# Both phases of a two-layer kernel in halves of d_ff, seven products for eight in three of the four, and converted weights kept in DRAM

## The chip, the cores and the metric

The kernel runs on one core of one Trainium2 chip. The metric is the device time of one execution in microseconds (us), as the median of several runs; smaller is better. The engines are TensorE (PE; PEld is its loading of the stationary operand), VectorE (DVE), ScalarE (ACT), GpSimd (POOL) and SyncE (SP), which issues nearly all DMAs.

## The reference

Three stages follow one another: sparse attention, then two two-layer networks with different activations. All is float32; the weights come as float64, two 32-bit words each.

```python
q, k, v: (4, 8, 576, 64)     # batch, heads, positions, head size
mask_local   = (rel >= 0) & (rel < 32)                     # heads 0 to 3; rel = query - key position
mask_strided = (rel >= 0) & (key % 32 == query % 32)       # heads 4 to 7
x = softmax(where(mask, q @ k.T / 8, -1e9)) @ v            # then (2304, 512)

h = x @ w_in                                               # first phase, w_in (512, 2048)
g = h where h >= 1, 0 where h <= -1, else (h + 1) ** 2 / 4
x = g @ w_out                                              # w_out (2048, 512)

h = x @ w2_in                                              # second phase, same shapes
out = (s * relu(h) ** 2 + b) @ w2_out
```

## The kernel before

**Tiles.** Tokens go in nine blocks `j` of 256 (`g` counts the blocks of both phases, 0 to 17), d_ff in eight pairs `p` of 128-wide tiles. One *step* is one layer of one block and one pair. The first layer (`layer1`, L831) takes 24 matmuls of 256 columns into one PSUM bank `h`: four chunks of d_model, two d_ff tiles, three products each, since every operand is split into a rounded part and a residual (`xh`, `xl`; `w[:, 0]`, `w[:, 1]`; `gh`, `gl`) and high x high, high x low and low x high are summed. `activate` (L846) makes `g`. The second layer of the first phase (`layer2`, L937) takes 24 more, with the weights stationary, into `y`, so its result comes out with d_model on the partitions. The second phase uses `layer2_fast` (L893): Strassen's scheme in Winograd's form on 2x2 blocks, seven products for eight, 21 matmuls a step. For it `combine` (L871) makes four sums `s1` to `s4` of quarters of `h` and `u`, `w_combine` (L707) the four differences `t1` to `t4` of the weights, and `finish_fast` (L908) adds up the seven results.

**Order of the work.** `PASSES` (L62) lists the block passes: (block, first pair, end). The second layer runs `LAG` = 2 pairs behind the first. In the first phase all sixteen d_ff tiles' weights are in SBUF; blocks 0 and 1 go two pairs at a time, blocks 2 to 5 in one pass of eight, blocks 6 to 8 in two halves. The second phase goes in halves: all its blocks with pairs 0 to 3, then with pairs 4 to 7. Where a block has several passes, the first phase stores each pass's result in DRAM (`x2`, L397) and adds them when the second phase loads them (`x_split`, L788); the second phase stores partial sums (`sums`) and adds them in `finish_fast`. Sixteen attention units (batch, pair of heads) run beside this from the step numbers in `STARTS` (L51); units listed in `MEMORY` borrow weight rooms.

**Weights.** Each of the 64 tiles is loaded by one DMA (`w_load`, L657) and converted from float64 by three VectorE operations (`w_bits`, L682) and split by one ScalarE copy and one subtraction (`w_parts`, L700). `W_TIMES` and `W_NEXT` (L73) give the step at which each tile's load is due; `pump` (L753) waits for free rooms (SBUF buffers of 4 KB a partition).

**Who sets the order.** The class `Order` records every operation with a due time (`nc.now`, in steps) and then orders them itself with prices of its own, each engine's queue separately; at each moment the ready operation with the earliest due time goes next. So all operations stand in the profile under the one line that issues them, L381, and are told apart by tile names. Every queue runs in its order: an operation that waits holds up all behind it on its engine, SyncE's DMAs included.

Of the kernel before, what the change touches and what calls it, by code (L numbers as in the profile page):

```python
# [67 lines left out]


AGAIN = (6, *range(9, 16))  # L70


W_TIMES = {0: (-7, 1.9, 3), 1: (7.9, 1.9, 2.6)}  # L73
W_NEXT = {0: (113, 1.4), 1: (150, 3.2)}
W_AHEAD, W_RETRY, W_GAP = 3, 0.5, 1.2
# [3 lines left out]
U_BANKS, W_BANKS = ("a0", "a1", "a2", "a3"), ("a3", "a2", "a1", "a0")  # L79
W_BANKS_FAST, Y_BANKS_FAST = ("a3", "a2"), ("y0", "y1", "a0", "a1")  # L80
# [35 lines left out]
class Order:  # L116
# [4 lines left out]
    BANKS = ("h0", "h1", "y0", "y1", "a0", "a1", "a2", "a3")  # L121

    def __init__(self, nc):
        self.nc, self.ops, self.place, self.count, self.seen, self.first = nc, [], {}, {}, {}, {}
        self.past = set()
        self.filler = []
        self.choices, self.uses = {}, {}
        self.tiles, self.shadow = {}, bacc.Bacc("TRN2", target_bir_lowering=False, num_devices=1)
        self.now = 0.0

        self.in_line, self.line = False, None
        for e in self.ENGINES:
            setattr(self, e, Order.Engine(self, e))
# [56 lines left out]
    def record(self, engine, op, args, kw):  # L190
# [28 lines left out]
        self.line = i if self.in_line else None  # L219
        deps.discard(i)  # L220
# [7 lines left out]
    def price(self, engine, op, out, aps, kw):  # L228
# [5 lines left out]
        if engine == "tensor":  # L234
            n = out.free_size()
            if op == "transpose":
                return n * 0.00085
            if aps[1].dtype == F32:
                return max(0.0255, 0.0004 * n)
            return n * 0.000453  # L240
        if engine == "scalar":
            return (0.17 if psum else 0.2) + 0.00083 * n + 0.09 * (isinstance(kw.get("bias"), bass.AP) + ("accum_out" in kw))
        if engine == "vector":
            return 0.15 + (0.00052 if self.fast(op, aps) else 0.00104) * n
        if engine == "gpsimd":
            return (0.25 + 0.0019 * n if n <= 512 else 0.12 + 0.0017 * n) if op != "memset" else 0.04 + 0.0009 * n
# [138 lines left out]
def attention_moe_moe(ctx, tc, q, k, v, w1_in, w1_out, w2_in, w2_out, s_in, b_in, consts, out):  # L385
# [10 lines left out]
    x2 = [  # L396
        [nc.tile(dram, [P, NC, N], F32, f"x2_{j}_{i}") for i in range(sum(g == j for g, _, _ in PASSES))] for j in range(NBLK)  # L397
    ]
# [11 lines left out]
    turns = [0]  # L410
# [11 lines left out]

    def put(b, copy, o, i):
# [6 lines left out]
    class Unit:  # L430


        def __init__(self, b, pair, mem, quick=False, natural=False):
            self.b, self.pair, self.mem, self.quick, self.natural = b, pair, mem, quick, natural
# [3 lines left out]
            self.id = f"{b}_{pair}"  # L438

# [45 lines left out]
        def load_v(self):  # L485
            queue = nc.gpsimd if self.quick and not self.strided else nc.sync
# [108 lines left out]
        def smul(self):  # L595
            nc.vector.tensor_tensor(
# [57 lines left out]
    rooms, half_rooms, halves = [], [], {}  # L654
    wt, wraw, wtags, reserved, used = {}, {}, {}, {}, {}

    def w_load(ph, f, x):  # L657
        w = ((w1_in, w1_out), (w2_in, w2_out))[ph][x]
        if ph == 0:
            tag = f"w{f}_{x}"  # L660
        else:
            tag = reserved[f // 2].pop(0) if x else rooms.pop(0)
        wtags[ph, f, x] = tag

        r = wraw[ph, f, x] = nc.tile(sb, [P, DM, 2], I32, tag=tag, name=f"wr{ph}_{f}_{x}")
        if x == 0:
            nc.sync.dma_start(
                out=r.rearrange("p (c m) w -> p c (m w)", m=P),
                in_=w[:, 2 * f * P:2 * (f + 1) * P].rearrange("(c p) m -> p c m", p=P),
            )  # L670
        else:
            nc.sync.dma_start(out=r.rearrange("p m w -> p (m w)"), in_=w[f * P:(f + 1) * P, :])


    wc = {}

    def w_abs(ph, f, x):
        c = nc.bank(ps, W_BANKS if now[0] < 2 * NP * NBLK - 4 else W_BANKS_FAST, f"c{ph}_{f}_{x}", "c")
        nc.scalar.activation(out=c, in_=wraw[ph, f, x][:, :, 1].bitcast(F32), func=AF.Abs, scale=REBIAS)
        wc[ph, f, x] = c  # L680

    def w_bits(ph, f, x):  # L682
        c, r = wc[ph, f, x].bitcast(I32), wraw[ph, f, x]
        o = wc[ph, f, x] = nc.tile(sb, [P, DM], I32, tag="wc", bufs=WC_BUFS, name=f"wc{ph}_{f}_{x}")
# [22 lines left out]
    def w_combine(p):  # L707

        r0, r1 = [wc.pop((1, 2 * p + f, 1)).bitcast(F32) for f in range(2)]
        b11, b12, b21, b22 = r0[:, :HM], r0[:, HM:], r1[:, :HM], r1[:, HM:]  # L710

        r = wraw[1, 2 * p + 1, 1].bitcast(F32).rearrange("p m w -> p (m w)")
# [4 lines left out]
        t, tags = {}, {0: wtags[1, 2 * p, 1], 1: reserved[p][2], 2: reserved[p][0], 3: reserved[p][1]}  # L717
        for i, c, eng in ((2, u, nc.vector), (3, w, nc.gpsimd), (0, r1, nc.gpsimd), (1, b11, nc.vector)):
            o = t[i] = w_room(tags[i], f"w1_{p}_{i}", c.free_size())
            nc.scalar.activation(out=o[:, 0], in_=c, func=AF.Copy)  # L720
            eng.tensor_tensor(out=o[:, 1], in0=c, in1=o[:, 0].bitcast(F32), op=ALU.subtract)
        b21, b22 = t[0][:, :, :HM], t[0][:, :, HM:]
        t1, t3, t2, t4 = t[2][:, :, :HM], t[2][:, :, HM:], t[3][:, :, :HM], t[3][:, :, HM:]
        wt[1, p] = dict(b11=t[1], b21=b21, b22=b22, t1=t1, t2=t2, t3=t3, t4=t4)
        rooms.append(wtags[1, 2 * p + 1, 1])
        used[1, p] += tags.values()

    def w_free(ph, p):
        for tag in used.pop((ph, p)):
            (half_rooms if tag in halves else rooms).append(tag)  # L730

    def plan_w(f):
        for x in range(2):
            first, step, apart = W_TIMES[f // (NF // 2)]
            t = first + step * (f % (NF // 2)) + apart * x
            at(t - W_AHEAD, w_load, 0, f, x)
            at(t, w_abs, 0, f, x)
            at(t, w_bits, 0, f, x)
            at(t + 0.3, w_parts, 0, f, x)

    todo = [
        (W_NEXT[p // HP][0] + W_NEXT[p // HP][1] * (4 * (p % HP) + 2 * x + f), (1, 2 * p + f, x))
        for p in range(NP) for x in range(2) for f in range(2)
    ]
    loaded = [0]

    def half_split(tag):
# [371 lines left out]
```

## Time and profile before

| | |
|---|---|
| median of 3 runs | 914.93 us (913.59 to 916.2) |
| the profiled execution's own time | 914.73 us |
| its span, first to last instruction | 913.0 us |
| mean granted TensorE clock | 0.987 |
| TensorE, VectorE, ScalarE, GpSimd busy | 886.8, 523.3, 495.9, 414.1 us |
| DMA | 103.37 MB, mean 113 GB/s |

The shares of busy time are means over unlike stretches, so what an engine's time is worth is read from a stretch and from who waits there. Matmuls overlap in the records, so their spacing, not their mean duration, is their cost.

### The profile page before, as it was taken

What the parts mean: (1) busy time and instruction counts of PE and PEld (TensorE: products, weight loads), DVE (VectorE), ACT (ScalarE), POOL (GpSimd) and SP (SyncE); (2) the same over time, 40 slices, a digit from 0 to 9 for tenths busy, and PEclk for the clock granted to TensorE, in tenths of its full rate; (3) what the DMA queues carried; (4) which work ended last, traced back from release to release, by engine and by line L of the source; (5) the groups of instructions that cost most, each with busy time, mean ns of one, the idle gap of its engine ahead of it and who ended that gap; (6) DMA issues with size and microseconds to landing.
All of it is one profiled execution on the core that took longest, in us unless ns stands there. A gap on an engine that the chain in (4) does not pass through costs nothing.

```text
span 913.0 us, 22147 instructions
## 1 busy us (share of the span) xinstructions
PE 886.8 (97%) x8922; PEld 872.8 (96%) x8922; DVE 523.3 (57%) x1057; ACT 495.9 (54%) x1097; POOL 414.1 (45%) x350
## 2 busy tenths in 40 slices
PE   8987999999999999999999999999999999999996
PEld 7987999999999999999999999999999899999996
DVE  2787686443443342333696888744457965455455
ACT  2676677545444443233554687665666655555553
POOL 4174454122222112222354577987645665545544
PEclk9999799999999999999999999999999999999999
DMA  9899322422222211002635743445134332222211
GB/s 161 258 300 309 89 75 71 103 52 52 64 52 63 53 61 70 1 24 70 209 127 172 232 140 116 145 136 183 70 115 164 98 129 99 94 93 93 94 47 47
DMA packets 122966, 103.37 MB, mean 113 GB/s; under 512 B 84272, under 2 KB 100976, under 8 KB 122864
## 3 DMA queue, kind: packets, MB, share of 16 engines
q1 hardware_dynamic: 122352, 100.85, 36.7%
q0 software_dynamic: 512, 1.11, 0.6%
q8 instruction: 70, 1.15, 0.5%
q14 instruction: 32, 0.26, 0.1%
HBM read 73.63 MB, written 28.31 MB: 112 GB/s over the span
## 4 chain that ended last, share of the span: by engine, by line
PE 87%; DMA 3%; DVE 3%; ACT 2%; POOL 2%; issue 2%; SPq 0%; POOLq 0%; DVEq 0%; ACTq 0%
PE h L381 40%; PE y L381 38%; PE s L381 3%; PE o L381 2%; PE idle L381 2%; DMA wr<-in_moe_w_out_dram 1%; POOL gl L381 1%; PE t L381 1%; PE p L381 1%; DMA x<-o 1%; DMA wr<-in_moe_w_in_dram 1%; DVE o L381 1%; ACT u L381 1%; POOL w L381 1%; DMA mem<-in_q_dram 1%
## 5 line engine op out<-in xcount | busy, mean ns | idle before, releaser
L381 PE MATMUL h<-xh,w 128*128 128x256 f32 x2304 | 436.3, 281 | 5.7 <-ACT xh L381 3.0
L381 PEld LDWEIGHTS h<-xh,w 128*128 128x128 f32 x2304 | 364.0, 189 | 7.4 <-ACT xh L381 3.1
L381 PE MATMUL h<-xl,w 128*128 128x256 f32 x1152 | 323.2, 281 | 0.0
L381 PE MATMUL y<-g,w 128*128 128x256 f32 x1728 | 221.9, 283 | 5.7 <-DVE o L381 5.7
L381 PEld LDWEIGHTS h<-xl,w 128*128 128x128 f32 x1152 | 217.4, 189 | 0.3
L381 PEld LDWEIGHTS y<-g,w 128*128 128x128 f32 x1728 | 210.8, 190 | 6.6 <-DVE o L381 5.8
L381 POOL TENSOR_TENSOR g<-u,g 128x512 fp32r<-128x512 f32 x72 | 95.4, 1324 | 246.3 <-ACT g L381 148.3
L381 PE MATMUL y<-w,g 128*128 128x256 f32 x864 | 158.2, 281 | 1.0 <-ACT w L381 1.0
L381 ACT ACTIVATE u<-h 128x512 f32<-128x512 f32 x144 | 85.9, 598 | 119.0 <-DVE h L381 55.5
L381 PEld LDWEIGHTS y<-w,g 128*128 128x128 f32 x864 | 132.3, 188 | 1.3 <-ACT w L381 1.3
L381 DVE TENSOR_SCALAR u<-h 128x512 f32<-128x512 f32 x72 | 49.6, 689 | 132.1 <-PE h L381 126.7
L381 POOL TENSOR_TENSOR gl<-u,g 128x384 fp32r<-128x384 f32 x72 | 75.1, 1043 | 100.8 <-ACT g L381 95.1
L381 PE MATMUL y<-w,gl 128*128 128x256 f32 x432 | 120.7, 281 | 0.0
L381 POOL TENSOR_TENSOR gl<-s,g 128x512 fp32r<-128x512 f32 x72 | 97.8, 1358 | 33.8 <-ACT g L381 31.5
L381 ACT ACTIVATE u<-u,half 128x512 f32<-128x512 f32 x72 | 52.0, 722 | 108.2 <-DVE u L381 106.9
L381 ACT ACTIVATE g<-u 128x512 fp32r<-128x512 f32 (+1 forms) x144 | 83.2, 578 | 36.5 <-DVE u L381 30.3
L381 DVE TENSOR_SCALAR h<-h,sbt 128x512 f32<-128x512 f32 x72 | 58.6, 814 | 69.6 <-ACT h L381 69.6
L381 POOL TENSOR_TENSOR w<-wc,w 128x512 fp32r<-128x512 f32 x56 | 74.0, 1327 | 43.5 <-ACT w L381 38.8
L381 PEld LDWEIGHTS y<-w,gl 128*128 128x128 f32 x432 | 81.0, 188 | 0.1
L381 DVE TENSOR_TENSOR o<-y,o 128x256 f32<-128x256 f32 x120 | 46.4, 415 | 41.5 <-PE y L381 40.0
L381 DVE TENSOR_TENSOR u<-h,u 128x512 f32<-128x512 f32 x72 | 49.3, 685 | 23.2 <-ACT u L381 23.1
L381 ACT ACTIVATE g<-s 128x512 fp32r<-128x512 f32 x72 | 45.3, 629 | 14.8 <-DVE s L381 14.8
(91 smaller groups left out, 995.9 us busy)
## 6 DMA issues: line engine op xcount, KB each, us to landing
wr<-in_moe_w_in_dram SPq DMA_DIRECT2D x32, 512.0 KB
wr<-in_moe_w_out_dram SPq DMA_DIRECT2D x32, 512.0 KB
x<-o SPq DMA_DIRECT2D x36, 256.0 KB
scratch<-x SPq DMA_DIRECT2D x18, 512.0 KB
y<-o SPq DMA_DIRECT2D x22, 256.0 KB
scratch<-y SPq DMA_DIRECT2D x11, 512.0 KB
out_dram<-o SPq DMA_DIRECT2D x18, 256.0 KB
xhd<-xh SPq DMA_DIRECT2D x8, 512.0 KB
```

The lines of the kernel that those rows point to most:

```text
L381: getattr(getattr(self.nc, engine), op)(*args, **kw)
```

## The change

The first phase too goes in halves of d_ff: a half `hp` is 0 or 1 in the first phase and 2 or 3 in the second, and in each half every block takes one pass of pairs 0 to 3 (blocks 0 and 1 of half 0 two pairs at a time). Of the 288 steps each half has 72.

- Half 0 keeps eight products, but with `g` stationary and the weights moving, 512 columns a matmul: 12 for 24. Half 1 uses `layer2_fast`, as the second phase does, so `combine` and `w_combine` run there too, and the max of the activation is written to `h`.
- Results of the first phase now have tokens on the partitions. Half 0's are stored as partial sums in DRAM; half 1's `finish` loads and adds them (on GpSimd), transposes 32x32 blocks on VectorE, and stores them in `x2` in pieces of 128 bytes, 72 DMAs of 64 KB in all. The second phase loads a block in four DMAs, with no addition; its `w_in` loads come in four DMAs of 32 partitions to match.
- At the start only half 0's weights are loaded. Of each later half the pairs in `FAR` (2 and 3) are converted early, stored in DRAM (`w_store`) and fetched (`fetch`) when rooms come free; pairs 0 and 1 stay in SBUF. `W_NEXT` sets the due steps.
- `xh` and `xl` of every block are kept in DRAM after their first making and loaded for the second half.
- Attention starts are packed into steps up to 37 (before 76); all units use the quick form (one exponential per unit on ScalarE, with subtraction and sum on VectorE; before four units), and the product with 1/sum is GpSimd's.
- The recording class has other prices for some operations, and keeps weight loads behind the newest matmul (`held`).

```diff
-STARTS = (-14, -11.2, -13.5, -11.7, 1.8, 8, 14.7, 21.4, 31, 37, 43, 48, 58, 64, 70, 76)
+STARTS = (-14, -11.2, -13.5, -11.7, -6.5, -2.6, 1.3, 5.2, 9.1, 13, 16.9, 20.8, 25, 29, 33, 37)
...
 PASSES = (
-    [(g, p, p + 2) for p in range(0, NP, 2) for g in range(2)] + [(g, 0, NP) for g in range(2, 6)]
-    + [(g, 0, HP) for g in (6, 7, 8)] + [(g, HP, NP) for g in (7, 8, 6)]
-    + [(g, 0, HP) for g in (*range(11, 15), 9, 10, 15)] + [(g, p, p + 2) for p in (0, 2) for g in (16, 17)]
-    + [(g, HP, NP) for g in (16, 17, *range(9, 16))]
+    [(0, j, p, p + 2) for p in (0, 2) for j in (0, 1)] + [(0, j, 0, HP) for j in range(2, 9)]
+    + [(1, j, 0, HP) for j in (7, 8, *range(7))] + [(2, j, 0, HP) for j in (7, 8, *range(7))]
+    + [(3, j, 0, HP) for j in (5, 6, 7, 8, *range(5))]
 )
...
-W_TIMES = {0: (-7, 1.9, 3), 1: (7.9, 1.9, 2.6)}
-W_NEXT = {0: (113, 1.4), 1: (150, 3.2)}
...
+W_FIRST, W_STEP, W_APART = -10, 3.8, 1.9
+W_NEXT = {
+    (1, 2): (24, 2.4), (1, 3): (33, 2.4), (1, 0): (42, 2.4), (1, 1): (51, 2.2), (2, 2): (60, 2.4), (2, 3): (84, 4), (2, 0): (100, 4),
+    (2, 1): (116, 4), (3, 2): (150, 4), (3, 3): (166, 4), (3, 0): (182, 4), (3, 1): (198, 3),
+}
...
+    def w_store(key, tag, t):
+        d = far[key] = nc.tile(dram, [P, 2, t.shape[2]], F32, "far" + "_".join(map(str, key)))
+        nc.sync.dma_start(out=d, in_=t.bitcast(F32))
+        w_back(tag)
...
+    def fetch():
+        while fetches:
+            hp, p, x = fetches[0]
+            if any(h <= hp for _, (h, *_) in todo) or (hp, p, 1 if not x else 3, *"c"[:x]) not in far:
+                break
+            if (hp, 0) not in used or nc.now < 2 * HP * NBLK * hp - 12:
+                break
+            if x and (len(rooms) < 3 or not half_room()) or len(rooms) < 2:
+                break
...
+            nc.vector.tensor_tensor(out=h if hp else u, in0=h, in1=u, op=ALU.max)
+        if hp:
...
+            combine(hp, j, p, u, h, gt)
...
+                y, first, last = ys[hp, j][i], p == p0 and f == 0, p == p1 - 1 and f == 1
+                nc.tensor.matmul(y, gh, t[:, 0], start=first, stop=False)
+                nc.tensor.matmul(y, gh, t[:, 1], start=False, stop=False)
+                nc.tensor.matmul(y, gl, t[:, 0], start=False, stop=last)
...
+                nc.vector.transpose(turned[:, i], o[i])
+                for a in range(0, P, 32):
+                    nc.sync.dma_start(
+                        out=x2[j][:, :, i * P + a:i * P + a + 32],
+                        in_=turned[a:a + 32, i].rearrange("p (b t) -> p b t", t=32),
+                    )
```

How the order moves shows at three places. The first is SyncE's queue around the first stores of results. Before, blocks 0 and 1 store theirs (`x2_0`, `x2_1`) behind loads of weight tiles (`wr`, the last numbers d_ff tile and matrix):

```order
L381 DMA wr0_13_1_1151<-in_moe_w_out_dram 128x1024
L381 DMA wr0_15_0_1163<-in_moe_w_in_dram 128x4x256
L381 DMA wr0_14_1_1184<-in_moe_w_out_dram 128x1024
L381 DMA wr0_15_1_1206<-in_moe_w_out_dram 128x1024
L381 DMA x2_0_0_1230<-o0_0_1214 128x512
L381 DMA x2_0_0_1230<-o0_1_1234 128x512
L381 DMA x2_1_0_1426<-o1_0_1422 128x512
L381 DMA x2_1_0_1426<-o1_1_1430 128x512
```

In the change, block 0's partial sum (`y0_0`) is stored among loads of attention inputs (`raw`, `v`); the last `wr` of half 0 stands 24 rows ahead of that store:

```order
L389 DMA mem_raw0_1_3_1161<-in_q_dram 96x6x64 x2
L389 DMA y0_0_1_1282<-o0_0_0_0_1276 128x512
L389 DMA y0_0_1_1282<-o0_0_0_1_1287 128x512
L389 DMA mem_raw1_1_3_1332<-in_k_dram 96x6x64 x2
L389 DMA yr0_0_2_1355<-y0_0_1_1282 128x1024
L389 DMA mem_v1_1_3_1375<-in_v_dram 18x6x64
```

The weight loads have gone from just ahead of the first stores. The second place is VectorE's queue in the first phase, where a block is finished (`o`, block 5 before). Before, one copy from `y`, among clips and maxes of later steps:

```order
L381 TENSOR_SCALAR u6_0_5481<-h6_0_5451 128x512
L381 TENSOR_TENSOR u6_0_5481<-h6_0_5451,u6_0_5481 128x512
L381 TENSOR_SCALAR u6_1_5537<-h6_1_5509 128x512
L381 COPY o5_0_5552<-y5_0_5127 128x512
L381 TENSOR_TENSOR u6_1_5537<-h6_1_5509,u6_1_5537 128x512
L381 TENSOR_SCALAR u6_2_5601<-h6_2_5567 128x512
```

In the change, half 1, where block 3 is finished (`o1_3`) beside steps of block 4 (`h1_4`) and conversions of half 2's weights (`c2`, `wr2`, `wc2`):

```order
L389 TENSOR_TENSOR o1_3_0_0_6338<-y1_3_0_1_6094,o1_3_0_1_6313 128x256
L389 SCALAR_TENSOR_TENSOR wc2_1_0_0_6344<-wr2_1_0_0_6113,c2_1_0_0_6173 128x512
L389 TENSOR_TENSOR h1_4_1_6270<-h1_4_1_6270,u1_4_1_6331 128x512
L389 TENSOR_TENSOR o1_3_0_1_6313<-y1_3_0_0_6068,o1_3_0_1_6313 128x256
L389 TENSOR_TENSOR o1_3_0_1_6313<-y1_3_0_1_6094,o1_3_0_0_6338 128x256
L389 TENSOR_SCALAR c2_1_1_0_6328<-c2_1_1_0_6328 128x512
L389 TENSOR_TENSOR s1_4_1_6384<-h1_4_1_6270,u1_4_1_6331 128x128 x2
L389 TENSOR_TENSOR s1_4_1_6384<-s1_4_1_6384,h1_4_1_6270 128x128
L389 TENSOR_TENSOR o1_3_0_0_6338<-y1_3_0_2_6103,o1_3_0_0_6338 128x256
L389 TENSOR_TENSOR s1_4_1_6384<-h1_4_1_6270,s1_4_1_6384 128x128
L389 TENSOR_TENSOR o1_3_0_0_6338<-y1_3_0_1_6094,o1_3_0_0_6338 128x256
L389 TENSOR_TENSOR o1_3_0_1_6313<-y1_3_0_2_6103,o1_3_0_1_6313 128x256
```

Four sums `s` a step, seven operations a block and the conversions now stand in one queue. The third place is TensorE's queue at the boundary between the phases. Before, block 6's second layer and then the first step of block 2 in the second phase (`h11`), with more of block 6 to follow:

```order
L381 MATMUL y6_1_6979<-g6_5_6931,w0_10_1_1786 128x256 x3
L381 MATMUL y6_1_6979<-g6_5_6931,w0_11_1_1892 128x256 x3
L381 MATMUL y6_1_6979<-g6_5_6931,w0_10_1_1786 128x256 x3
L381 MATMUL y6_1_6979<-g6_5_6931,w0_11_1_1892 128x256 x3
L381 MATMUL h11_0_7084<-xh11_6752,w1_0_0_6044 128x256
L381 MATMUL h11_0_7084<-xl11_6774,w1_0_0_6044 128x256
```

In the change, block 6's last products (`y1_6`) and the first step of block 7 in the second phase (`h2_7`):

```order
L389 MATMUL y1_6_0_2_7022<-wf1_3_1_2_4244,gl1_6_3_7144 128x256
L389 MATMUL y1_6_0_2_7022<-wf1_3_1_0_4347,g1_6_3_7138 128x256 x2
L389 MATMUL h2_7_0_7179<-xh2_7_7165,w2_0_0_0_5735 128x256
L389 MATMUL h2_7_1_7181<-xh2_7_7165,w2_1_0_0_6355 128x256
L389 MATMUL y1_6_0_2_7022<-wf1_3_1_0_4347,gl1_6_3_7144 128x256
L389 MATMUL h2_7_0_7179<-xl2_7_7177,w2_0_0_0_5735 128x256
L389 MATMUL h2_7_0_7179<-xh2_7_7165,w2_0_0_0_5735 128x256 x2
```

All but one of block 6's products now stand ahead of the first matmul that needs `xl2_7`.

## Rows read from the trace of the kernel before

**Rows 1.** The page: the span, and busy time of TensorE (PE) and the others.
```profile
span 913.0 us, 22147 instructions
PE 886.8 (97%) x8922; PEld 872.8 (96%) x8922; DVE 523.3 (57%) x1057; ACT 495.9 (54%) x1097; POOL 414.1 (45%) x350
```

**Rows 2.** The chain of waits, 350 to 450: start, length, what.
```profile
377.38 2.80 PE h L381 x24
```

**Rows 3.** What TensorE waited for: total us, times, longest.
```profile
PE y L381 <- DVE o L381: 6.1, 2, 5.7
```

**Rows 4.** The chain of waits, 83 to 93.
```profile
83.71 8.36 DMA x<-o
92.09 0.70 DVE o L381
```

**Rows 5.** Stretches, 84 to 102: length, then busy us per engine, clock, DMA share, GB/s.
```profile
84.00:94.00 10.00, 3.30 (x20) 2.59 (x20) 5.26 (x10) 3.73 (x7) 2.49 (x2) 0.67 0.71 241
94.00:100.00 6.00, 6.00 (x89) 5.71 (x88) 4.69 (x9) 3.85 (x8) 3.74 (x3) 0.50 0.27 87
100.00:102.00 2.00, 2.00 (x16) 2.00 (x15) 0.69 (x1) 0.90 (x3) 0.00 (x0) 0.72 0.30 68
```

**Rows 6.** TensorE in order of time, 130.8 to 132.4: start, us, instruction.
```profile
130.82 0.39 PE L381 MATMUL s<-narrow 128*128 128x512 bf16 x1
131.14 1.10 PE L381 MATMUL s<-qk,qk 64*32 64x64 f32 x64
132.17 0.20 PE L381 MATMUL s<-narrow 128*128 128x64 bf16 x1
132.31 0.32 PE L381 MATMUL s<-qk,qk 64*32 64x64 f32 x8
```

**Rows 7.** Stretches, 41 to 54 (columns as in rows 5).
```profile
41.00:50.00 9.00, 5.31 (x111) 4.33 (x110) 6.63 (x12) 6.62 (x16) 4.44 (x5) 1.00 1.10 339
50.00:54.00 4.00, 4.00 (x23) 4.00 (x22) 4.00 (x7) 2.93 (x7) 2.55 (x2) 0.58 1.18 236
```

**Rows 8.** VectorE by operation and shape: count, busy us, mean ns, idle before it.
```profile
L381 DVE TENSOR_SCALAR u<-h 128x512 f32<-128x512 f32 x72 | 49.6, 689 | 132.1 <-PE h L381 126.7 <-POOL g L381 5.2
L381 DVE TENSOR_TENSOR u<-h,u 128x512 f32<-128x512 f32 x72 | 49.3, 685 | 23.2 <-ACT u L381 23.1
L381 DVE TENSOR_TENSOR s<-h,u 128x128 f32<-128x128 f32 x144 | 35.1, 284 | 31.3 <-ACT u L381 29.5 <-POOL w L381 0.6
L381 DVE TENSOR_TENSOR o<-y,o 128x256 f32<-128x256 f32 x120 | 46.4, 415 | 41.5 <-PE y L381 40.0 <-ACT g L381 1.4
L381 DVE STREAM_TRANSPOSE qk<-raw 128x576 f32<-128x576 f32 x16 | 15.6, 1008 | 11.9 <-PE o L381 10.8 <-ACT g L381 1.0
L381 DVE TENSOR_SCALAR c<-c 128x512 int32<-128x512 int32 x64 | 43.3, 691 | 15.0 <-ACT c L381 15.0
L381 DVE TENSOR_TENSOR wr<-wc,wr 128x256 f32<-128x256 f32 x8 | 8.0, 997 | 0.0
L381 DVE TENSOR_TENSOR wr<-wr,wc 128x256 f32<-128x256 f32 x8 | 4.6, 569 | 0.0
L381 DVE TENSOR_TENSOR w<-wr,w 128x512 fp32r<-128x512 f32 x8 | 7.8, 976 | 0.2 <-ACT w L381 0.2
L381 DVE TENSOR_TENSOR halves<-wc,halves 128x256 fp32r<-128x256 f32 x6 | 3.4, 574 | 0.0
L381 DVE TENSOR_TENSOR xl<-scratch,xh 128x512 fp32r<-128x512 f32 x9 | 12.4, 1382 | 0.6 <-ACT xh L381 0.6
```

**Rows 9.** Stretches with a full VectorE (columns as in rows 5).
```profile
450.00:470.00 20.00, 20.00 (x174) 20.00 (x173) 19.97 (x29) 13.61 (x24) 11.64 (x9) 1.00 0.43 141
705.00:740.00 35.00, 31.49 (x257) 30.41 (x256) 31.02 (x65) 22.06 (x42) 24.02 (x20) 1.00 0.28 91
```

**Rows 10.** Traffic: stretch 690 to 700, and the page on DMA packets.
```profile
690.00:700.00 10.00, 10.00 (x87) 10.00 (x87) 6.46 (x19) 6.13 (x13) 4.62 (x4) 1.00 0.78 288
DMA packets 122966, 103.37 MB, mean 113 GB/s; under 512 B 84272, under 2 KB 100976, under 8 KB 122864
```

More of the change, by code (lines that the diff above doesn't have):

```diff
@@ L394, in attention_moe_moe @@
     sbt = nc.tile(sb, [P, 2], F32, "sbt")
-    x2 = [
-        [nc.tile(dram, [P, NC, N], F32, f"x2_{j}_{i}") for i in range(sum(g == j for g, _, _ in PASSES))] for j in range(NBLK)
-    ]
+    x2 = [nc.tile(dram, [32, DM // 32, N], F32, f"x2_{j}") for j in range(NBLK)]
     now = [0, 0]
@@ L409, in attention_moe_moe @@
     filled = [0] * B
-    turns = [0]
+    turns, scratch = [0], []
     def x_room(name, *dims):
@@ L485, in load_v @@
         def load_v(self):
-            queue = nc.gpsimd if self.quick and not self.strided else nc.sync
+            queue = nc.gpsimd if self.early and not self.strided else nc.sync
             vh = self.heads(v)
@@ L675, in attention_moe_moe @@
[L675 to L684, printed above, removed]
+    rooms = [f"w{n}" for n in range(ROOMS)]
@@ new lines, in attention_moe_moe, with half_room, half_split @@
+    half_rooms = [f"b{n}" for n in range(HALF_ROOMS)]
+    wt, wraw, wtags, wc, reserved = {}, {}, {}, {}, {}
+    used, halves = {}, {}
+    def half_room():
+        if not half_rooms and len(rooms) > 3:
+            tag = rooms.pop(0)
+            half_split(tag, nc.tile(sb, [P, 2, 2, HM], F32R, tag=tag, name=f"halves_{tag}"))
+        return half_rooms
+    def half_split(tag, t):
+        for i in range(t.shape[1]):
+            halves[tag, i] = t[:, i]
+            half_rooms.append((tag, i))
@@ L685, in w_bits, with w_abs @@
+    def w_abs(*tile):
+        c = nc.bank(ps, W_BANKS if now[0] < 2 * HP * NBLK - 8 else W_BANKS_FAST, "c%d_%d_%d_%d" % tile, "c")
+        nc.scalar.activation(out=c, in_=wraw[tile][:, :, 1].bitcast(F32), func=AF.Abs, scale=REBIAS)
+        wc[tile] = c
+    def w_bits(*tile):
+        c, r = wc[tile].bitcast(I32), wraw[tile]
+        o = wc[tile] = nc.tile(sb, [P, DM], I32, tag="wc", bufs=WC_BUFS, name="wc%d_%d_%d_%d" % tile)
         nc.vector.tensor_scalar(
@@ L725, in w_combine @@
[L725 to L739, printed above, removed]
+        wt[hp, p] = dict(b11=t[1], b21=b21, b22=b22, t1=t1, t2=t2, t3=t3, t4=t4)
@@ L744, in attention_moe_moe, with later @@
     ]
     loaded = [0]
-    def half_split(tag):
-        t = nc.tile(sb, [P, 2, 2, HM], F32R, tag=tag, name=f"halves_{tag}")
-        for i in range(2):
-            halves[tag, i] = t[:, i]
-            half_rooms.append((tag, i))
-    def pump():
-        while todo and todo[0][0] <= nc.now and nc.now >= loaded[0] + W_GAP:
-            ph, f, x = tile = todo[0][1]
-            p = f // 2
-            if x and f % 2 == 0:
-                if not half_rooms and len(rooms) > 4 and p >= HP:
-                    half_split(rooms.pop(0))
-                if len(rooms) < 4 or not half_rooms:
+    def later(fn, hp, *args):
+        nc.now += W_LATE * (hp > 0)
+        fn(hp, *args)
+        nc.now -= W_LATE * (hp > 0)
@@ L761, in pump @@
+    def pump():
+        fetch()
+        while todo and not (fetches and fetches[0][0] < todo[0][1][0] and todo[0][1][1] not in FAR) and todo[0][0] <= nc.now:
+            if todo[0][1][0] and nc.now < loaded[0] + W_GAP:
+                break
+            hp, p, f, x = tile = todo[0][1]
+            kept = SPARE if nc.now < STARTS[-1] + 7 else 0
+            if hp and x and not f:
+                if len(rooms) < 3 + kept or not half_room():
                     break
-                reserved[p] = [rooms.pop(0) for _ in range(4)] + [half_rooms.pop(0)]
-            elif not x and not rooms:
+                reserved[hp, p] = [rooms.pop(0) for _ in range(3)] + [half_rooms.pop(0)]
+            elif hp and not x and len(rooms) <= kept or not hp and not rooms:
```

422 lines of the change are left out of this document (234 added, 188 removed).

## Prediction

> **What bounds the kernel now.** I read the page first. TensorE is busy 97% of a span of 913.0 us [rows 1]. So the kernel is bound by the number of TensorE columns, plus the few places where TensorE stands still. The chain of waits gives the price of work: where nothing disturbs it, a layer of one pair of d_ff tiles, 24 matmuls of 256 columns, takes 2.80 us, or 0.1167 us a matmul [rows 2]. The waits of TensorE then show what it stood still for: the longest is 5.7 us, for VectorE's `o` [rows 3]. It is not VectorE's doing. In the chain the copy `o<-y` begins when four stores `x<-o` have landed, 8.36 us after their issue [rows 4]: they stand in the DMA queue behind weight tiles. By stretches [rows 5], TensorE is idle 6.7 us between 84 and 94, and the granted clock is 0.50 (1.2 GHz) from there to about 101, some 8.2 us at half rate, which loses 4.1 us more. That stall costs 10.8 us.
>
> **The change part by part**, against the profiled execution (914.73 us, span 913.0; the median of the runs is 914.93, so nothing is corrected).
>
> *Products.* The order of TensorE's instructions has 3240 second-layer matmuls of 256 columns before; the change has 2268 of 256 and 432 of 512, worth 864 of 256. That is 108 fewer, all on the path: 108 x 0.1167 = **-12.6 us**.
>
> *Wide matmuls.* The first half of the first phase now moves 512 columns per stationary tile instead of twice 256. No fp32r matmul of 512 columns is in this trace. From below: the same time per column, no gain. From above: the 2.4 GHz clock moves 512 columns in 0.2133 us, and 432 x (0.2333 - 0.2133) = -8.7 us. Between them stand bf16 rows [rows 6]: from a matmul of 512 columns to the next start is 0.32 us, from one of 64 columns 0.14 us, so 448 more columns cost 0.18 us, 0.40 ns a column, within the rounding the 0.417 of a 2.4 GHz clock, where 0.1167 us over 256 is 0.456. With 0.1167 + 256 x 0.42 ns = 0.224 a pair saves 0.009, and 432 x 0.009 = **-3.9 us**; I take it because those rows are the only ones of that width.
> The Trainium skill (TensorE: Matmul & The Clock Gate, "Back-to-back issue gap") gives an isolated gap of columns / 2.4 GHz plus 2.5 ns: 109.2 ns for 256 columns and 215.8 for 512. The 116.7 ns of [rows 2] do not agree. By it the two terms above would be -11.8 and -1.1, and the total about 903.
>
> *The stall at 84.* Its cause is gone: of the first phase's weights only half is loaded at the start, and in SyncE's queue no weight tile stands just ahead of the first stores of partial sums (first order listing). The credit is the whole **-10.8 us**; if another backlog takes its place it is 0.
>
> *Startup.* TensorE's gaps at 41 to 50 (3.7 us) and the half clock to 54 [rows 7] come from ScalarE doing six copies of the attention's output and weight conversions before the first `xh`. The same six copies and nearly as many conversions ahead of them remain. Zero; the bounds are a gain of all of it (3.7 + 2.1 = 5.8 us) and as much loss, since the attention's product with 1/sum moves to GpSimd, ahead of the `xl` that the first matmuls need.
>
> *VectorE in the second half of the first phase.* This is where the change adds most [rows 8]. Per pair of d_ff tiles: 0.689 (clip), 0.685 (max) and four sums `s` of 0.284, together 2.51 us; 36 of them, 90.4 us. Finishing a token block: seven operations of 0.415 and two 32x32 transposes (1.008 x 512/576 = 0.90 each), 4.70 us, nine times, 42.3. Converting twelve tiles of the next half at three operations of 0.69 each: 24.8. Four combines, each four subtractions (0.57 to 1.00, say 0.78), one of 0.976 and one of 0.57: 18.7. Sum 176 us. TensorE needs 36 x (24 + 21) x 0.1167 = 189 us there (21.0 a block). So VectorE must be busy 93% of the time while TensorE waits on it directly: for the PSUM bank of `h`, which the `s` sums still read, and for the `y` banks, which the finish empties. In the second order listing those operations stand among the conversions. How full VectorE can be without starving TensorE has two rows [rows 9]. At 450 to 470 it is busy 19.97 of 20 and TensorE loses nothing, but there only two VectorE operations stand on a step's path. At 705 to 740, with the same `s` sums, finishes and conversions mixed, it reaches 31.0 of 35 (88.6%) and TensorE stands still 3.5 us. The second is the nearest: 176/0.886 = 199, **+10 us**. Lower end 0 (the first row); upper end if the conversions cannot slip out of their 44 planned steps: from step 84 to 128 5.5 blocks need 5.5 x (4 x 2.51 + 4.70) + 24.8 + 14.0 (three combines) = 120 us, 135 at that ceiling, against 5.5 x 21.0 = 115.5 of TensorE: +20.
>
> *Phase boundary.* The third listing shows TensorE running out of other work: the last 60 products of block 6 stand ahead of the second phase's first matmul, which needs a residual `xl` that VectorE makes behind two operations of block 6's finish. 2 x 0.415 + 1.382 + 0.2 for the handover [rows 8] = **+2.4 us**; upper end another 10.8, when the clock falls too.
>
> *Hidden.* Attention now ends near step 43 instead of 82, and its exponentials with accumulators on ScalarE become subtractions and reductions on VectorE. In the first half VectorE has only two operations (clip and max) on a step, 1.37 us of 5.6, and this fits beside them; if it did not, it would be a second stretch like 705 to 740, 3.5 us. The stored and fetched weight pairs are DMA time beside TensorE's, unless (c) holds.
>
> Sum: 914.7 - 12.6 - 3.9 - 10.8 + 10 + 2.4 = 899.8, say **900**.
>
> **The rivals.**
> (a) *No new wait, wide matmuls at the array's rate.* 914.7 - 12.6 - 8.7 - 10.8 = **883**. For it: 450 to 470, and the phase 2 stretches where TensorE is busy throughout. Against: 705 to 740.
> (b) *One backlog, or VectorE at its upper end.* The stall's credit is lost once, or conversions cannot slip: about **910**. For it: nearly all loads and stores still pass one queue, SyncE's, in order.
> (c) *Slower: the DMA queue backs up at the half changes.* The far pairs 2 and 3 of the next half are fetched only when rooms come free, with the last use of pair 0; from there to the first matmul of pair 2 TensorE has three first layers (2.80 each) and three second layers (2.45): 15.8 us. If the fetch lands later at two of the three half changes, each costs what the stall at 84 cost: 900 + 2 x 10.8 = **922**; at three, 932. It decides once more than 15.8 us of traffic, 4.5 MB at 288 GB/s [rows 10], stands ahead of a fetch. For it: traffic grows from 103 MB to about 151 (counted from the order), 4.7 of it in pieces of 128 bytes. Against: only 1 MB has to land in that time, and at 690 to 700 the queues moved 288 GB/s with TensorE busy throughout [rows 10].
> The Trainium skill (DMA: Bandwidth & Descriptors, "Specifications") asks for 512 bytes or more per piece, below which a write becomes a read and a write; no run here shows what the 128-byte stores cost.
> That the change doesn't do what it says is ruled out by the count of matmuls.
>
> **How the numbers follow.** The forecast has 0.42, (a) 0.26, (b) 0.18, (c) 0.14. A measurement here can tell 0.3%, 2.7 us. The forecast and (a) are faster; (b) straddles the bound, half and half; (c) is slower. So faster 0.77, same 0.09, slower 0.14. The range goes from 880, just below (a), to 918, above (b) and short of (c); what it leaves out is (c) and a gain at startup on top of (a), some 0.18.
>
> **What would show it.** Right: the `y` groups count 108 fewer columns of 256; 512-column matmuls start 0.22 us apart; no stall at 80 to 100 and no clock below 1.00 there; in the stretch of the second half, about 200 us long, VectorE near 90% busy and TensorE's waits naming `s` and `o`. Wrong: TensorE idle under 3 us in that stretch (then (a)); waits of TensorE for `wf` tiles or for `xh` loads at the half changes (then (c)); a clock of 0.5 anywhere after the start.

## The result and the profile after

The change is slower, by half a per cent: 920.93 us (917.36 to 923.54) against 915.27 (913.59 to 917.85) on the same chip, ratio 1.0055 with a 95% interval of 1.0028 to 1.0081. The forecast was 900, the range 880 to 918. The profiled execution took 921.14 us. The page of the change, which answers to [rows 1] and to the packets in [rows 10]:

```profile
span 919.4 us, 21651 instructions
PE 880.8 (96%) x8354; PEld 843.7 (92%) x8354; DVE 581.7 (63%) x1295; ACT 505.0 (55%) x935; POOL 481.8 (52%) x410
...
DMA packets 174565, 154.73 MB, mean 168 GB/s; under 512 B 124864, under 2 KB 141568, under 8 KB 174464
```

TensorE has 6 us less to do, and the span is 6.4 longer: it stands still for some 12 us more. To see where, I divide both traces into quarters by the first-layer matmuls (3456 in each; a quarter begins with every 864th, the fourth ends with the last matmul), so that equal work is compared.

| quarter | before | change | difference | forecast |
|---|---|---|---|---|
| first, without attention still to do | 300.5 + 8.3 | 308.9 | +0.1 | -14.7 (stall, wide matmuls) |
| second, without attention | 211.4 - 8.3 | 214.8 | +11.7 | -0.2 (products, VectorE, boundary) |
| third | 193.0 | 191.7 | -1.3 | 0 |
| fourth | 200.9 | 196.9 | -4.0 | 0 |

(8.3 us is what TensorE's matmuls after 300.5 that belong to neither `h` nor `y` take before, by their spacing.) So the misses are in the first two quarters: the first came out 14.8 us above the forecast, the second 11.9, and the other two 5.3 below. In the second, which is half 1, the starts of the nine blocks are 21.8, 21.2, 26.8, 22.6, 24.9, 23.6, 23.6, 21.1 and 29.0 us apart; undisturbed blocks of half 2 have 21.3. The first eight lose 15.2 us and the last, at the boundary between the phases, 7.7.

Stretches of the change (columns as in [rows 5]): the start, half 1, the boundary, and 6 us in which SyncE issues a block's transposed results.

```profile
0.00:40.00 40.00, 32.69 (x562) 30.24 (x563) 15.06 (x40) 17.62 (x37) 14.58 (x23) 1.00 0.89 174
40.00:60.00 20.00, 14.71 (x233) 13.31 (x232) 11.98 (x23) 14.00 (x30) 11.90 (x11) 0.83 1.06 323
60.00:80.00 20.00, 16.29 (x177) 14.55 (x178) 12.66 (x25) 12.29 (x25) 9.94 (x8) 0.66 0.97 235
80.00:102.00 22.00, 22.00 (x247) 19.41 (x246) 16.38 (x30) 13.20 (x26) 11.79 (x10) 1.00 0.46 111
...
309.00:519.00 210.00, 201.50 (x1638) 198.12 (x1637) 148.76 (x355) 108.94 (x191) 121.57 (x103) 0.98 0.55 157
...
491.00:497.00 6.00, 6.00 (x54) 6.00 (x53) 5.22 (x13) 3.42 (x7) 3.64 (x4) 1.00 0.69 158
...
519.00:536.00 17.00, 11.35 (x68) 10.44 (x68) 7.86 (x17) 5.66 (x11) 5.79 (x5) 0.80 0.75 225
```

The same stretches of the start, before:

```profile
0.00:40.00 40.00, 36.26 (x589) 34.26 (x590) 17.35 (x42) 18.62 (x39) 10.60 (x20) 0.96 0.85 187
40.00:60.00 20.00, 16.21 (x188) 14.90 (x186) 17.61 (x29) 15.23 (x30) 12.94 (x10) 0.91 1.11 329
60.00:80.00 20.00, 20.00 (x234) 19.51 (x233) 15.81 (x27) 15.01 (x42) 12.84 (x11) 1.00 1.02 322
80.00:102.00 22.00, 15.30 (x156) 14.30 (x155) 14.38 (x26) 10.43 (x21) 7.94 (x8) 0.69 0.62 173
```

The stall at 84 is gone, as forecast: 22.00 of 22 busy, clock 1.00. But TensorE now stands still 16.3 us up to 80, where it stood still 7.5 before; by 102 the two are 16.3 and 14.2, and the low clock (0.66 after, 0.69 before) has only moved ahead. Up to 80 TensorE's longest waits for transfers name the attention's inputs; before, up to 102, `v` is not among its waits and `q` stands at 0.6 us:

```profile
PE o L389 <- DMA v<-in_v_dram: 3.2, 1, 3.2
PE t L389 <- DMA mem_raw<-in_q_dram: 3.2, 2, 2.9
```

In half 1 VectorE is busy 148.76 of 210, 71%, not near 90, and what TensorE waited for from 309 to 519 is first of all ScalarE's `g`, not VectorE's `o` and `s`:

```profile
PE y L389 <- ACT g L389: 3.8, 3, 1.8
PE y L389 <- DVE o L389: 2.0, 2, 1.1
PE h L389 <- DVE s L389: 1.5, 3, 0.6
```

The chain of waits of the change (start, length, what) shows a layer of 512-column matmuls, one of half 1's stalls, the boundary, and two fast layers:

```profile
164.77 2.81 PE y L389 x12
...
358.10 8.08 DMA wr<-in_moe_w_in_dram
...
366.20 0.62 ACT c L389
366.82 0.52 ACT u L389
...
367.43 0.53 ACT g L389
...
368.03 1.01 POOL gl L389
...
520.39 2.59 DMA scratch<-x
...
523.01 0.64 ACT xh L389
...
523.71 1.28 POOL xl L389
...
525.04 7.76 PE h L389 x46
...
614.50 2.87 PE h L389 x24
617.37 2.48 PE y L389 x21
```

At 358 a weight tile of half 2 is still on its way. ScalarE's next operation is the copy `c<-wr` of that tile, so it stands still until 366.18, with `u` and `g` of the running step behind the copy; TensorE gets its `gl` at 369. Such landings of 7 to 8 us stand in the chain at 358, 384 and 431, and the waits of ScalarE in half 1 count them:

```profile
ACT c L389 <- DMA wr<-in_moe_w_in_dram: 9.6, 3, 4.2
ACT c L389 <- DMA wr<-in_moe_w_out_dram: 5.7, 3, 3.0
```

One reason why they land late is in SyncE's queue (its DMA instructions, count at the end; `x<-scratch` is a store of transposed results, `scratch<-x` a load of the second phase), here before the stall at 366 and at the boundary:

```profile
347.91 5.34 SPq L389 DMA_DIRECT2D x<-scratch  x8
...
355.90 3.02 SPq L389 DMA_DIRECT2D wr<-in_moe_w_in_dram  x4
...
513.88 3.13 SPq L389 DMA_DIRECT2D scratch<-x  x2
517.11 2.58 SPq L389 DMA_DIRECT2D x<-scratch  x4
519.74 1.08 SPq L389 DMA_DIRECT2D scratch<-x  x2
```

The eight stores of a block's transposed results take SyncE 5.3 us to issue, and the loads stand behind them; at the boundary the second phase's first block is loaded (`scratch<-x`) in part behind such stores and lands at 522.98.

### The profile page after: what moved, and what is told of

It is laid out like the page before. It is cut to its first block, busy times and chain, and to the rows that moved or that the text cites. A ratio compares the mean times of both kernels' runs of the same rounds, so it can differ in the third digit from the quotient of the medians.

```text
span 919.4 us, 21651 instructions
## 1 busy us (share of the span) xinstructions
PE 880.8 (96%) x8354; PEld 843.7 (92%) x8354; DVE 581.7 (63%) x1295; ACT 505.0 (55%) x935; POOL 481.8 (52%) x410
## 3 DMA queue, kind: packets, MB, share of 16 engines
q0 software_dynamic: 512, 1.11, 0.6%
## 4 chain that ended last, share of the span: by engine, by line
PE 64%; DMA 6%; DVE 3%; SPq 3%; issue 2%; POOL 2%; ACT 2%; ACTq 0%; POOLq 0%; DVEq 0%
PE h L389 33%; PE y L389 30%; SPq L389 3%; DMA wr<-in_moe_w_out_dram 3%; DMA wr<-in_moe_w_in_dram 3%; POOL gl L389 1%; ACT u L389 1%; DVE o L389 1%; DVE u L389 1%; DVE c L389 1%; ACT c L389 1%; DVE s L389 1%; PE s L389 0%; PE o L389 0%; ACT g L389 0%
## 5 line engine op out<-in xcount | busy, mean ns | idle before, releaser
L389 PE MATMUL h<-xh,w 128*128 128x256 f32 x1440 | 277.4, 285 | 6.2 <-ACT xh L389 3.8
L389 PEld LDWEIGHTS h<-xh,w 128*128 128x128 f32 x1440 | 230.8, 191 | 9.2 <-ACT xh L389 4.0
L389 PE MATMUL h<-xl,w 128*128 128x256 f32 x720 | 204.0, 283 | 0.3 <-POOL xl L389 0.3
L389 PE MATMUL h<-xh,wf 128*128 128x256 f32 x864 | 165.3, 281 | 1.5 <-DVE s L389 1.5
L389 PEld LDWEIGHTS h<-xh,wf 128*128 128x128 f32 x864 | 137.6, 189 | 2.1 <-issue 2.1
L389 PE MATMUL y<-wc,g 128*128 128x256 f32 x666 | 124.1, 284 | 2.0 <-DVE o L389 2.0
L389 PE MATMUL y<-wf,g 128*128 128x256 f32 x666 | 121.4, 281 | 0.0
L389 PE MATMUL h<-xl,wf 128*128 128x256 f32 x432 | 121.3, 281 | 0.0
L389 PE MATMUL y<-w,g 128*128 128x512 f32 x432 | 110.8, 399 | 0.2 <-ACT w L389 0.2
L389 PEld LDWEIGHTS y<-wc,g 128*128 128x128 f32 x666 | 103.9, 192 | 2.3 <-ACT w L389 2.3
```

The source lines that it names most:

```text
L389: getattr(getattr(self.nc, engine), op)(*args, **kw)
```

## The experiments

The theory after this reading: the 21 us between forecast and result are waits on transfers that come later than the order assumes (tiles in half 1, the first block of the second phase, attention inputs at the start), and 4 us of wide matmuls. The rival is the prediction's own mechanism, a VectorE too full for the chain from `h` to `gl`. Ratios are to the kernel before on the same chip; the last column is the difference to the kernel that was edited, in us, from the ratios.

| run | edit of | median | ratio (95%) | difference |
|---|---|---|---|---|
| land6 | change | 906.61 | 0.9919 (0.9899 to 0.9939) | -12.4 |
| x_early | change | 921.26 | 1.0083 (1.0059 to 1.0107) | +2.6 |
| eight_half1 | change | 912.79 | 0.9980 (0.9955 to 1.0004) | -6.9 |
| narrow | change | 925.21 | 1.0125 (1.0096 to 1.0153) | +6.4 |
| x2_long2 | change | 902.09 | 0.9866 (0.9831 to 0.9901) | -17.3 |
| x2_long8 | change | 909.65 | 0.9949 (0.9922 to 0.9977) | -9.7 |
| both_early | land6 | 901.25 | 0.9862 (0.9826 to 0.9898) | -5.2 |
| start4 | both_early | 912.83 | 0.9979 (0.9956 to 1.0001) | +10.7 |
| no_xd01 | both_early | 901.60 | 0.9842 (0.9818 to 0.9866) | -1.8 |
| starts_b1 | both_early | 900.74 | 0.9833 (0.9810 to 0.9855) | -2.7 |
| x2_act | both_early | 939.68 | 1.0261 (1.0229 to 1.0293) | +36.5 |
| eight_best | starts_b1 | 906.85 | 0.9908 (0.9875 to 0.9942) | +6.9 |
| land0_3 | starts_b1 | 899.74 | 0.9837 (0.9800 to 0.9874) | +0.4 |
| land0 | starts_b1 | 908.11 | 0.9925 (0.9897 to 0.9954) | +8.4 |

**land6.**

```diff
-                end = dma + 1.2
+                end = dma + 1.2 + W_LAND * self.place.get(o.tensor.name, [""] * 6)[5].startswith(("wr1", "wr2", "wr3"))
```

> One number of the planner: it takes a weight tile of the three later halves to land 6 us later than before, so it orders the copies `c<-wr` later in ScalarE's queue and the VectorE operations behind them. The work is the same. Late tiles (the theory): in the second half of the first phase each of some five stalls of TensorE begins with a copy that waits for a tile's landing while the activation's copies stand behind it; the nine blocks lose 16 us there, and this run wins most of it, 6 to 16 us below the change, some 910. VectorE full (the rival, the mechanism of the prediction): what VectorE has to do is unchanged, so the time stays within 2 us.

It gains 12.4 us and is faster than before. Here is half 1 up to 500, ahead of the boundary, and all that TensorE waited for from 309 to 500:

```profile
308.70:500.00 191.30, 190.92 (x1595) 189.44 (x1594) 146.84 (x346) 106.01 (x186) 118.92 (x100) 1.00 0.60 170
```

```profile
PE h L389 <- DVE s L389: 0.3, 1, 0.3
```

ScalarE waits for no tile there. VectorE has the same work in less time, 77% busy, and TensorE loses 0.4 us in 191. The first eight blocks take 172.0 us, for 185.7 in the change. So most of the 15 us of the eight blocks were copies that stood in ScalarE's queue before their tiles had landed, and VectorE's load is no bound.

**eight_half1.** `hp > 1` for `hp` in `activate`, `layer2` and `finish`, and the second half's `w_out` tiles stored and fetched as they are:

```diff
-        if hp:
+        if hp > 1:
             layer2_fast(hp, j, p0, p1, p)
```

> The second half of the first phase with eight products, as the first half: no sums `s`, no seven-operation finish, no differences of weights; 108 x 2 more columns-of-256 matmuls less the half already there, that is 36 steps x 3 = 108 matmuls of 256 columns more, +12.6 us of TensorE. VectorE full: the 16 us that the nine blocks lose go with VectorE's work, so the time falls by 16 - 12.6, some 3 us below the change. Late tiles: the tiles to be converted beside that half are as many as before, and so are their waits; the time rises by 9 to 13 us.

Neither number came: 6.9 us are gained, where the rival said 3 and the theory a loss. The first eight blocks of half 1 take 22.4 us each (the last 23.3) and lose nothing, though ScalarE waits longer for tiles than in the change (24.8 us against 15.3):

```profile
ACT c L389 <- DMA wr<-in_moe_w_in_dram: 16.7, 5, 5.4
...
ACT c L389 <- DMA wr<-in_moe_w_out_dram: 8.1, 4, 3.5
```

So a late tile alone does not stop TensorE. With eight products the step's chain (two operations of VectorE and two of ScalarE) may be short enough to make up for such a wait before the second layer, two pairs later, needs `g`; with the four sums and the second split behind it, it is not. land6 and this run together show that it takes both, a late tile and the seven-product form. Which part of that form matters, the length of its chain or VectorE's load beside it (109 us busy in half 1 here, 149 in the change), is not separated: this run takes away both.

**x2_long2 and x2_long8.** The change with its transposed results stored in long rows:

```diff
-                for a in range(0, P, 32):
-                    nc.sync.dma_start(
-                        out=x2[j][:, :, i * P + a:i * P + a + 32],
-                        in_=turned[a:a + 32, i].rearrange("p (b t) -> p b t", t=32),
-                    )
+                nc.sync.dma_start(out=x2[j][:, i * DM:(i + 1) * DM], in_=turned[:, i])
```

x2_long8 has instead, in the loop:

```diff
+                    nc.sync.dma_start(out=x2[j][a:a + 32, i * DM:(i + 1) * DM], in_=turned[a:a + 32, i])
```

> The change, but the transposed results are stored in rows of 2 KB, two DMAs a block for eight, so the second phase reads its tokens in the wrong places (the output is not the reference's; the work is the same but for these stores). Queue (the theory): SyncE has 0.6 us where it had 5 a block, and no pieces of 128 bytes; the boundary's 8 us fall to 2 or less and part of the second half's late tiles come in time: 6 to 14 us below the change. Rival: the stores are hidden, and the boundary waits for block 6's finish itself: within 2 us.

> As x2_long2, but in eight DMAs a block as in the change, of 32 rows of 2 KB each (the output is not the reference's). If the number of DMAs is what costs, the issue time and the stalls stay: within 2 us of the change. If the pieces of 128 bytes are what costs (in SyncE's issue time, or on the DMA engines), it gains as much as x2_long2, 6 to 14 us.

Both gain: long rows in as many DMAs 9.7 us, in a quarter as many 17.3. So the pieces cost by themselves, as does the number of DMAs; neither rival holds alone. (The recording class prices a transfer by its rows, so the order behind these stores can differ in both runs.) A store's issue by SyncE (shortest, median, longest in ns), in the change and in x2_long8:

```profile
L389 SPq DMA_DIRECT2D x<-scratch x72: 556/627/1393, 347.9 to 537.4; - x72
```

```profile
L389 SPq DMA_DIRECT2D x<-scratch x72: 302/419/1767, 345.8 to 520.8; - x72
```

So pieces of 128 bytes cost SyncE half as much again per DMA. On the DMA engines the stretch 491 to 497 above has 158 GB/s at a share of 0.69, where [rows 10] have 288 at 0.78; what else moves in the two differs, so this points to a cost there and does not measure it. By the packet records of the change a piece of 128 bytes takes 13 ns in the median and one of 2 KB 84, that is 10 bytes a ns against 24. These stores are what makes more than half of the waits for tiles: in x2_long2 ScalarE waits 6.5 us for them in half 1, for 15.3, and the nine blocks lose 7.5 us (199.2 in all), for 22.9. The gain of 17.3 is nearly the 17.6 that land6 and both_early (below) win together over the change; no run has both, so whether they add up is open.

**x_early and both_early.**

```diff
-                if i == p1 - p0 + 1 and (nxt[0] // 2, nxt[1]) not in xs:
+                if i == (1 if nxt[0] == 2 and (hp, j) in ((1, 6), (2, 7)) else p1 - p0 + 1) and (nxt[0] // 2, nxt[1]) not in xs:
```

(x_early has the first of the two places only.)

> The second phase's first block is loaded four places earlier in the order, ahead of the finish of block 5 instead of behind it; nothing else. Queue (the theory): SyncE's queue holds the four loads behind eight stores of 128-byte pieces, each of which takes it some 0.63 us to issue; TensorE's stall at 519 to 533 with the half clock behind it, some 8 us, goes: 4 to 8 us below the change. Rivals: the stall is VectorE's (the residual `xl` behind the finish) or the fetched weights', and comes back a few us later: within 2 us.

x_early missed: its time is within the noise of the change. The stall at 519 is gone (the block takes 21.9 us), and the next block, whose load is behind block 6's stores, takes 28.2. The chain there:

```profile
537.60 0.62 SPq L389
...
545.16 3.74 DMA scratch<-x
```

> The planner's 6 us for weight tiles (as in the run land6) and both of the second phase's first blocks, 7 and 8, loaded four places earlier, ahead of the finishes of blocks 5 and 6. With block 7 alone moved, the stall went from block 7's load to block 8's, which stood behind block 6's eight stores. Queue (the theory): with both ahead the boundary costs 1 to 3 us instead of 8, so 4 to 7 us below land6, some 901. Rival: the stall moves on once more, to block 0 or to the sums that block 6's finish waits for: within 2 us of land6.

With both blocks ahead the boundary's block takes 22.5 us (28.7 in land6) and the next 22.8; 5.2 us are gained, as the queue theory had it.

**x2_act.**

```diff
-                    nc.sync.dma_start(
+                    nc.scalar.dma_start(
                         out=x2[j][:, :, i * P + a:i * P + a + 32],
```

> As both_early, with the 72 stores of 128-byte pieces issued by ScalarE and not by SyncE. Issue time (the theory): 0.63 us x 8 a block leave SyncE's queue, so what is left of the second half's and the boundary's loss (some 3 us each) goes, 2 to 5 us; ScalarE has room for 5 us a block. Rival: on ScalarE they wait for the transposes with the activation's copies behind them, and TensorE pays for it: slower by up to 10 us.

The rival holds, far above its number. ScalarE's waits in half 1 name the stores (a wait here is the time that their issue takes ScalarE, with what the issue waits for), and TensorE waits 19.5 us for `g`:

```profile
ACT g L389 <- DMA x<-scratch: 32.4, 4, 11.4
...
ACT u L389 <- DMA x<-scratch: 9.5, 3, 3.5
```

The Trainium skill (DMA: Bandwidth & Descriptors, the table row on spreading DMAs over engines) says that another issuing engine saves issue time but no bandwidth. Here what moved to ScalarE cost more than the issue time that left SyncE: 36.5 us net.

**narrow.**

```diff
-                nc.tensor.matmul(y, gh, t[:, 0], start=first, stop=False)
...
+                    for m in range(2):
+                        d = slice(m * HM, (m + 1) * HM)
+                        nc.tensor.matmul(y[:, d], l, r[:, d], start=first and not n and not m, stop=last and n == 2, **k)
```

> The first half's second layer in matmuls of 256 columns, two for each of 512, with the same operands: 864 for 432. Width counts (as the prediction had it, from the bf16 rows): 3.9 us slower than the change, up to 8.7. Width counts for nothing (twelve of 512 took 2.81 us in the chain of the change, twenty-four of 256 take 2.80): within 2 us of the change.

Not as clear as it was meant to be. Its layers take 0.03 to 0.07 us longer than the 2.81 of twelve wide ones, some 2 us in 36:

```profile
250.62 2.88 PE y L389 x24
...
256.34 2.84 PE y L389 x24
```

Most of the rest of the 6.4 stands in half 1, which the edit does not touch: it takes 4 us longer here (218.8 for 214.8). Against the kernel before, with the weights stationary and 2.80 a layer [rows 2], the wide form is worth nothing.

**The start: start4, no_xd01, starts_b1, land0_3, land0.**

```diff
-                free[e] = max(free[e], dma - DMA_AHEAD)
+                free[e] = max(free[e], dma - (DMA_AHEAD if t > 70 else 4))
```

> As both_early, and for the planner's first 70 us SyncE issues a transfer only when 4 us of transfers are ahead of it, not 12. So the second batch's `v` and `q` stand ahead of the last two pairs' weight tiles in its queue, not behind them. Queue at the start (the theory): the 12 us of backlog make the attention of the second batch wait (3.2 us for `v`, 2.9 for `q`), and the granted clock falls with it; 3 to 7 us below both_early. Rival: the 16 DMA engines are full from 40 to 70 whatever the order, so the wait moves from `v` to the weight tiles: within 2 us, or slower.

```diff
+        if ph == 0 and j < 2:
+            return
         xd[ph, j] = [nc.tile(dram, [P, NC, N], F32, f"x{p}d{ph}_{j}") for p in "hl"]
```

> As both_early, but `xh` and `xl` of blocks 0 and 1 are not stored in DRAM at the start; the second half loads block 2's in their place (so its output is not the reference's, the work is the same but for four stores of 512 KB). Volume (the theory): from 40 to 75 the DMA engines are full, and these 2 MB are what the change added there; without them the attention's inputs land up to 2.1 MB / 0.33 MB per us = 6 us earlier, and 3 to 6 us go. Rival: they stand behind the loads that TensorE waits for, so within 2 us of both_early.

```diff
-STARTS = (-14, -11.2, -13.5, -11.7, -6.5, -2.6, 1.3, 5.2, 9.1, 13, 16.9, 20.8, 25, 29, 33, 37)
+STARTS = (-14, -11.2, -13.5, -11.7, -3.5, -0.4, 2.6, 5.7, 9.1, 13, 16.9, 20.8, 25, 29, 33, 37)
```

> As both_early, with the second batch's four attention units started 0.5 to 3 places later (-3.5, -0.4, 2.6, 5.7 for -6.5, -2.6, 1.3, 5.2), so that their inputs ask for the DMA engines later. Packing (the theory): the attention was moved ahead into the stretch where the weights are loaded, and this undoes a part: 2 to 5 us below both_early. Rival: the second batch has to be done by the third block at place 16 all the same, and what is asked for later is waited for later: within 2 us, or slower.

In the line of land6, for land0_3 (land0 without the division):

```diff
-.startswith(("wr1", "wr2", "wr3"))
+.startswith("wr") / (2 if t < 70 else 1)
```

> As starts_b1, and the planner takes also the first half's weight tiles, loaded in the first 70 us, to land 3 us later. Late tiles at the start (the theory): between 40 and 66 ScalarE's copies `c<-wr` wait for landings with the attention's copies behind them, as in the second half; 2 to 5 us below starts_b1. Rival: the DMA engines are full there (share 1.0 or more), so what TensorE waits for comes no sooner in whatever order: within 2 us.

> As land0_3, with 6 us. Late tiles at the start: as much or a little more than land0_3. Rival: the weights of the first steps are converted later than they land, so it is 2 to 6 us slower than starts_b1.

The shorter backlog is 10.7 us worse. Two MB less gain nothing that the intervals can tell, nor does the later attention with its 2.7 us. Weight tiles expected 3 us later change nothing, 6 us later they cost 8.4. In the profile of starts_b1 the start is shorter (the second quarter begins at 304.9, for 308.4 in both_early), and in that of eight_best, with the same starts, too (304.0); but profiles whose start no edit touches range from 306.3 (x_early) to 308.9 (the change). The whole span of starts_b1 is as long as that of both_early (899.6 for 899.8), as the first block of half 2 takes 26.6 us for 22.8. Its stretches of the start:

```profile
0.00:40.00 40.00, 29.97 (x530) 27.47 (x530) 13.25 (x36) 14.09 (x29) 12.59 (x21) 0.96 0.86 186
40.00:60.00 20.00, 17.23 (x244) 15.40 (x243) 11.26 (x19) 14.89 (x35) 12.44 (x10) 0.85 1.08 288
60.00:80.00 20.00, 19.30 (x152) 17.31 (x153) 17.65 (x31) 15.11 (x28) 12.70 (x10) 0.98 0.79 216
```

In every kernel the DMA share is 1.0 or more from 40 to 60. None of the five runs shows that full DMA engines are what holds the start, and no_xd01, with two MB less, speaks against their volume as such. What holds it stays open.

**eight_best.** starts_b1 with the edit of eight_half1.

> As starts_b1, which has lost the stalls of the second half and of the boundary, with eight products in the second half of the first phase. It tells what seven products are worth there once nothing waits for late tiles. VectorE does not bind (the theory): with seven products VectorE is 77% busy there and TensorE loses about 1 us in 190, so the saving is nearly whole: 9 to 13 us slower than starts_b1, some 911. VectorE binds (the rival, the mechanism of the prediction, 10 us for 12.6): the saving is mostly eaten by VectorE's work, so eight products cost 1 to 4 us.

The time falls between the two, with runs far apart (897.9 to 910.84 among those behind the ratio). In the profiles half 1 takes 201.7 us against 194.1 with seven products: the saving there is 7.6 us. It is neither whole nor eaten.

The best version is starts_b1: 900.74 us, 1.7% faster than before, with three small edits of the change (when tiles are taken to land, where two blocks are loaded, four starts). By the intervals both_early and land0_3 cannot be told from it.

## Why the prediction was wrong

The forecast was 21 us too low: 14.8 at the start, 11.9 in half 1 with the boundary, less 5.3 behind it. Term by term:

*Products*, -12.6: too large. I took 2.45 + 2.80 us a step. Among fast layers the chain has 2.48 and up to 2.87, and an undisturbed block takes 21.3 us where one of eight products takes 22.4: 9 x 1.1 = 9.9 (7.6 came of it between eight_best and starts_b1). The spacing of second-phase blocks before (21.2, by the same starts) would have told it.

*Wide matmuls*, -3.9: wrong, the lower bound was right. Twelve of 512 columns take 2.81 us, 234 ns each, just twice the 116.7 of [rows 2]. The bf16 rows [rows 6] did not carry over. By the isolated gap of the Trainium skill (TensorE: Matmul & The Clock Gate, "Back-to-back issue gap") it would be 215.8 ns; the measurement does not agree.

*Stall at 84*, -10.8: the stall is gone with the cause that was named for it, and the credit is lost, as rival (b) had it. The step that failed is *Startup* at zero: it counted ScalarE's copies ahead of the first `xh` and not the attention's inputs, for which TensorE now waits up to 80 (`v` 3.2 us, `q` 3.2). The attention of the second batch was moved into a stretch whose DMA engines were full already (share 1.11 at 40 to 60 before); that this is why its inputs come late is not shown. Idle time up to 102 is 16.3 us for 14.2, and the first quarter is 0.1 us longer where 14.7 were to be won.

*VectorE in the second half*, +10: the loss (15.2) lies inside the range of 0 to 20, by a wrong mechanism, so its size was luck. The sum of 176 us was too high, since durations in the records overlap: the groups of half 1 add up to 166.4 us and VectorE is busy 148.76, and a transpose took 0.71, not 0.90:

```profile
L389 DVE STREAM_TRANSPOSE scratch<-o 128x512 f32<-128x512 f32 x16 | 11.4, 710 | 3.9 <-POOL o L389 3.9
```

The ceiling of 88.6% read from [rows 9] was never reached: land6 runs at 77% with 0.4 us lost. What set off the stalls was a ScalarE copy that waited in its queue for a late tile; where no tile was late, VectorE's work stopped almost nothing.

*Phase boundary*, +2.4: 7.7 us, between its bounds of 2.4 and 13.2, with 46 matmuls at a lower clock behind it (7.76 us, 0.169 each). I had `xl` wait behind VectorE's finish; GpSimd made it (1.28 us in the chain), and it waited for a load behind stores in SyncE's queue, as both_early shows.

*Later halves*: 5.3 us faster, forecast 0. The loss at 705 to 740 [rows 9] is not there any more. No run tells why.

Rival (c) had the right resource, the DMA queue, and the wrong place, so that its time of 922 came out is luck: not the fetches of the far pairs at the half changes, but weight tiles and the first blocks behind the 128-byte stores all through half 1. I held those stores for 4.7 MB in 151. Of the Trainium skill (DMA: Bandwidth & Descriptors, "Specifications") the prediction said that no run showed what pieces under 512 bytes cost. x2_long8 shows it: 9.7 us for the pieces alone. That short pieces cost agrees with the page; the read and write that it gives as the reason is not shown here.

## What to carry to other kernels

Price a transfer by its pieces and by the issuing engine's time, not by its bytes, and then see which loads stand behind it and which in-order engine stands behind those. Where an order is made ahead of time, an assumed landing that is too early puts a waiting copy in front of the running step; one number changed there won more here than the products saved. Sum an engine's busy time from stretches, not from mean durations.

## What the hardware showed that was not expected

A DMA of 64 KB in pieces of 128 bytes took SyncE 0.627 us to issue, in rows of 2 KB 0.419. Issued by ScalarE, the same stores, with what their issue waited for, held ScalarE up to 11.4 us at a time. By the packet records a piece of 128 bytes took 13 ns and one of 2 KB 84. Matmuls of 512 fp32r columns with a load of the stationary tile each start 234 ns apart, no faster per column than 256. VectorE operations overlap in the records of half 1 by about a tenth of their time (166.4 us by groups, 148.8 busy).
